# Float32 filling products, identity products tied to the dense products, and a new set of ranks in an mLSTM + two-MLP kernel

## The chip, the cores and the metric

The kernel runs on one core of a Trainium2 chip. The metric is the device time of one execution in microseconds, lower is better; the time of a kernel is the median of its runs. TensorE (PE in the profile) multiplies matrices, VectorE (DVE), ScalarE (ACT) and GpSimd (POOL) work element by element, SyncE (SP) issues the transfers. Each engine takes its own instructions strictly in their written order; between engines only semaphores order the work.

## The reference, cut to what matters

An mLSTM layer (4 batches, 8 heads, 768 steps, head size 40) is followed by two MLPs over 3072 tokens of width 320, each with 2048 hidden units:

```python
for t in range(S):
    m_new = max(f_gate + m, i_gate)
    C = exp(f_gate + m - m_new) * C + exp(i_gate - m_new) * outer(v, k)
    n = exp(f_gate + m - m_new) * n + exp(i_gate - m_new) * k
    y[t] = sigmoid(o_gate) * (C @ q) / max(abs(n @ q), 1)
x = y reshaped to (3072, 320)
h = x @ w_in;  g = where(h >= 1, h, where(h <= -1, 0, (h + 1)**2 / 4));  x = g @ w_out
h = x @ w2_in; g = maximum(h, 0)**2;                                     out = g @ w2_out
```

The MLP weights arrive as 64-bit floats and are cut into a high and a low part in the kernel.

## The kernel before

The sequence is cut into 24 chunks of 128 steps (4 batches, 6 chunks each). The attention of a chunk is: on PE the *spreads* (L507: the decay of four heads is copied to all partitions by float32 products with 36 rows), the *scores* (L540: float32, 40 rows), the *outer product* (L575) and the *reads* (L616: products of only 41 columns); on DVE the *decay* scans (L512), the *weighing* of the scores (L521), the state `C` (L585, L589), the normalised output `xn` (rc by L626 to L628, xn by L636); on ACT and POOL the gates and scalings. Then PE transposes `xn` (L655), ACT writes the high part of `xT` and DVE the low part `xTl` (L665).

Three chunks make a block, 8 blocks for each MLP. The weights are 16 tiles f. *Dense* products of a block and a tile f are `mm1` (L697, eight products of 384 columns) and, after ReLU, squaring and a split into g0 and g1 on ACT, DVE and POOL, `mm2` (L750, three products of 320 columns per chunk). The high and low parts of a weight tile are made from the raw words by ACT (L290), DVE (the shift pair L298 and L299, L303, L311) and ACT (L272). The low part of the weights is a subtraction; for the tiles in `PLO` it is done on PE as *identity products* (`plo`, twice per tile: L352 multiplies 352 float32 columns by the identity, L353 subtracts the high part), read back by ACT. All identity products write one tile in PSUM, `acc2`, which the third chunk's `mm2` needs after them.

In that same tile, *filling products* (L818, `idle`) multiply zeros. They compute nothing that is used. There are `FILL` of them, rank 1e6, so the plan puts one wherever PE would stand still.

What sets the order is a list scheduler, `Plan`. Every step has an engine (or a choice of engines), a rank and an assumed duration. The plan walks through time by its own durations, gives each free engine the ready step of lowest rank, and writes the instructions in that order. Tables of numbers set the ranks: `AT` (attention of the first nine chunks), `WAT` (weight tiles of the first MLP), `LEAD1` (later chunks), `GATE` and `GDMA` (gates of the later chunks and their transfers), `SIGL`, `WLEAD2`; `GLOV` lists the blocks whose low part of g is bound to DVE, other blocks may have it on POOL.

Of the kernel before, what the change touches and what calls it, by code (L numbers as in the profile page):

```python
# [10 lines left out]
BF16 = mybir.dt.bfloat16  # L11
# [24 lines left out]
class Plan:  # L36
# [5 lines left out]

    TABLE = {"sig": "sigmoid", "a1": "exp", "a2": "exp", "a3": "exp"}
# [14 lines left out]
    def order(self):  # L58
# [50 lines left out]
        while len(out) < n:  # L109
            t, eng = min((max(free[e], min(ready[i] for i in q)), e) for e, q in queue.items() if q)  # L110
            i = min((i for i in queue[eng] if ready[i] <= t), key=lambda i: (self.steps[i][1], i))
            queue[eng].remove(i)
            out.append((t, i))
            dur = self.steps[i][0][eng]
            want = self.TABLE.get(self.steps[i][2].__name__)
            if want and want != table:
                table, dur = want, dur + 1.3
            shared = eng == "P" or isinstance(dur, Shared)
            free[eng] = end = (max(t, port) if shared else t) + dur
            if shared:  # L120
                port = end
            for j in after[i]:
                left[j] -= 1
                lat = 0.02 if eng in self.steps[j][0] and eng != "SP" else self.LAT.get(eng, 0.1)
                ready[j] = max(ready[j], end + lat)
                if not left[j]:
                    enqueue(j)
# [34 lines left out]
AT = [-24, -19, -12, -4, 2, 2.0, 5.5, 8.5, 10.0]  # L162
WAT = [-13, -13.0, -7.5, -7.5, -3, -3.5, 1, 0.0, 6.0, 14.5, 16.0, 17.5, 16.5, 23.0, 22.5, 28.0]
LEAD1 = {3: [10.0, 11.5, 3.5], 4: [10.5, 6, 2.0], 5: [11.0, 8.0, 4.5], 6: [11.5, 7.5, 7.5], 7: [9.0, 5, 4.0]}
# [5 lines left out]
GATE = -14  # L170
FILL, FDUR = 140, 0.2
SIGL, GDMA = 3, 6
PLO = (0, 2, 3, 5, 6, 7)
WLEAD2 = (13, 0)
WDMA = 6
SGNV, LOV = (4, 4), (4, 0)
GLOV = (0, 1, 2, 3)
# [7 lines left out]
def kernel(  # L185
# [161 lines left out]
    def plo(f, rank, z):  # L347
        W, K = f"w{f}", (0, f)
        for i, (c0, c1) in enumerate(((0, WH // 2), (WH // 2, WH))):
# [10 lines left out]

            key = ("acc2", -1, f, i)
            last = plan.plo
            plan.plo = key + (1,)
            plan.add(T, rank, 0.85, sub, [("wt", K, 3), (W, 1), ("acc2", -1), ("nid", 0), last], [key])
# [446 lines left out]
    def idle_in():  # L811
        t_["idle"] = new("x2", [128, 512], BF16)
        nc.vector.memset(t_["idle"], 0.0)

    def idle(first):
        if first:
            t_["idle_ps"] = new("acc2", [128, 512])
        nc.tensor.matmul(out=t_["idle_ps"][:, WH // 2:], lhsT=t_["idle"][:, 0:128], rhs=t_["idle"][:, WH // 2:],  # L818
# [8 lines left out]
    for i in range(FILL):  # L827
        plan.add(T, -97 if i == 0 else 1e6, 0.22 if i < 30 else FDUR, lambda i=i: idle(i == 0),
# [105 lines left out]
```

## Time and profile before

| | us |
|---|---|
| median of 3 runs | 889.65 |
| lowest, highest | 886.09, 890.43 |
| the profiled execution | 887.01 |
| its span in the trace | 885.2 |
| PE busy in it | 868.0 (98%) |
| DVE, ACT, POOL busy | 468.3, 443.5, 333.1 |
| first dense product starts | 66.55 |

A busy PE is not a PE at its peak: the profile also has the clock that the chip granted to TensorE, as a share of 2.4 GHz, and only 1.00 and 0.50 (1.2 GHz) occur. In the views by stretch a mean between them is a mixture. The profile's page has the shares of the whole span; this case needs views of single stretches of its first 130 us, below.

### The profile page before, as it was taken

What the parts mean: (1) busy time and instruction counts of PE and PEld (TensorE: products, weight loads), DVE (VectorE), ACT (ScalarE), POOL (GpSimd) and SP (SyncE); (2) the same over time, 40 slices, a digit from 0 to 9 for tenths busy, and PEclk for the clock granted to TensorE, in tenths of its full rate; (3) what the DMA queues carried; (4) which work ended last, traced back from release to release, by engine and by line L of the source; (5) the groups of instructions that cost most, each with busy time, mean ns of one, the idle gap of its engine ahead of it and who ended that gap; (6) DMA issues with size and microseconds to landing.
All of it is one profiled execution on the core that took longest, in us unless ns stands there. A gap on an engine that the chain in (4) does not pass through costs nothing.

```text
span 885.2 us, 14965 instructions
## 1 busy us (share of the span) xinstructions
PE 868.0 (98%) x5782; PEld 845.9 (96%) x5782; DVE 468.3 (53%) x834; ACT 443.5 (50%) x919; POOL 333.1 (38%) x318
## 2 busy tenths in 40 slices
PE   7989999999999999999999999999999999999997
PEld 6868999999999999999999999999999999999997
DVE  4788888996765655345437788822222222222221
ACT  5255457764554554545568765533343434343433
POOL 3212431003221246446335666533333333333333
PEclk6789999999999999999999999999999999999999
DMA  6555562455441434334002333011010000000000
GB/s 202 186 180 163 172 176 88 142 171 165 124 125 47 120 106 122 108 100 124 28 10 68 131 121 126 10 34 41 26 33 26 25 26 16 8 16 9 16 9 23
DMA packets 55979, 75.72 MB, mean 86 GB/s; under 512 B 7252, under 2 KB 44792, under 8 KB 55908
## 3 DMA queue, kind: packets, MB, share of 16 engines
q1 hardware_dynamic: 55908, 74.77, 27.1%
q8 instruction: 45, 0.74, 0.3%
q14 instruction: 26, 0.21, 0.1%
HBM read 65.90 MB, written 8.85 MB: 84 GB/s over the span
## 4 chain that ended last, share of the span: by engine, by line
PE 93%; DVE 3%; DMA 2%; ACT 1%; issue 0%; SPq 0%; DVEq 0%; ACTq 0%
PE h L697 39%; PE acc L750 38%; PE v L616 4%; PE s L540 3%; PE s L655 2%; PE v L612 2%; PE v L575 1%; PE s L507 1%; PE acc L352 1%; DMA vko<-in_vko_dram 1%; DVE d L512 1%; DVE wt L303 1%; DMA qk<-in_qk_dram 0%; PE acc L818 0%; PE h L507 0%
## 5 line engine op out<-in xcount | busy, mean ns | idle before, releaser
L750 PE MATMUL acc<-w,g 128*128 128x320 f32 x2304 | 379.3, 311 | 0.0
L750 PEld LDWEIGHTS acc<-w,g 128*128 128x128 f32 x2304 | 350.6, 188 | 2.5 <-DVE o L778 0.3
L697 PE MATMUL h<-xTh,w 128*128 128x384 f32 x1280 | 351.8, 340 | 0.4 <-DVE r L715 0.3
L725 POOL TENSOR_TENSOR g<-r,g 128x384 fp32r<-128x384 f32 x192 | 204.9, 1069 | 285.0 <-ACT g L272 270.1
L697 PE MATMUL h<-xTl,w 128*128 128x384 f32 x768 | 258.8, 337 | 0.0
L697 PEld LDWEIGHTS h<-xTh,w 128*128 128x128 f32 x1280 | 233.4, 188 | 1.7 <-DVE r L715 0.9
L717 DVE TENSOR_TENSOR r<-r,h 128x384 f32<-128x384 f32 x128 | 70.8, 554 | 233.4 <-ACT r L704 233.3
L272 ACT ACTIVATE g<-r 128x384 fp32r<-128x384 f32 x256 | 133.5, 523 | 114.2 <-DVE r L717 64.3
L697 PEld LDWEIGHTS h<-xTl,w 128*128 128x128 f32 x768 | 144.8, 189 | 0.0
L704 ACT ACTIVATE r<-h 128x384 f32<-128x384 f32 x128 | 62.7, 490 | 137.3 <-PE h L697 104.6
L702 ACT ACTIVATE r<-h,half 128x384 f32<-128x384 f32 x128 | 74.1, 579 | 94.1 <-PE h L697 91.6
L715 DVE SCALAR_TENSOR_TENSOR r<-r,h 128x384 f32<-128x384 f32 x128 | 70.0, 548 | 72.6 <-ACT r L708 69.4
L708 ACT ACTIVATE r<-r 128x384 f32<-128x384 f32 x128 | 67.0, 523 | 3.0
L512 DVE TENSOR_TENSOR_SCAN d<-fb,csb 128x512 f32<-128x512 f32 x36 | 50.2, 1395 | 9.5 <-PE v L616 9.4
L547 POOL TENSOR_TENSOR vt<-vko,it 128x369 f32<-128x369 f32 x24 | 23.1, 961 | 80.0 <-PE v L616 53.6
L616 PEld LDWEIGHTS v<-vt,d 128*128 128x128 f32 x384 | 49.1, 197 | 0.5
L616 PE MATMUL v<-vt,d 128*128 128x41 f32 x384 | 49.2, 279 | 0.0
L569 POOL TENSOR_TENSOR kt<-vko,ws 128x360 f32<-128x360 f32 x19 | 16.8, 885 | 75.2 <-ACT ws L518 75.2
L725 DVE TENSOR_TENSOR g<-r,g 128x384 fp32r<-128x384 f32 x64 | 37.9, 594 | 8.7 <-ACT g L272 8.3
L521 DVE TENSOR_TENSOR d<-s,d 128x512 f32<-128x512 f32 x48 | 31.5, 680 | 17.8 <-PE s L540 17.6
L561 POOL TENSOR_TENSOR qt<-qh,ab 120x384 f32<-120x384 f32 x20 | 22.2, 1110 | 35.6 <-DMA ab<-a 28.3
L595 POOL TENSOR_TENSOR C<-cx,csb 120x369 f32<-120x369 f32 x16 | 15.4, 960 | 53.3 <-DVE cx L589 50.2
(76 smaller groups left out, 686.7 us busy)
## 6 DMA issues: line engine op xcount, KB each, us to landing
wraw<-in_wts_dram SPq DMA_DIRECT2D x32, 704.0 KB
vko<-in_vko_dram SPq DMA_DIRECT2D x24, 524.5 KB
fb<-f SPq DMA_DIRECT2D x18, 512.0 KB
qk<-in_qk_dram SPq DMA_DIRECT2D x48, 160.0 KB
x<-x SPq DMA_DIRECT2D x24, 192.0 KB
x<-o SPq DMA_DIRECT2D x24, 160.0 KB
out_dram<-o SPq DMA_DIRECT2D x24, 160.0 KB
qh<-in_qh_dram SPq DMA_DIRECT2D x20, 180.0 KB
```

The lines of the kernel that those rows point to most:

```text
L272: nc.scalar.activation(out=out, in_=in_, func=ACTF.Copy)
L512: nc.vector.tensor_tensor_scan(out=d.rearrange("p h t -> p (h t)"), data0=(z["fb"][a] if spr else z["fb"][:, 4 * a:4 * a + 4]).rearrange(" ...
L521: nc.vector.tensor_mul(out=z["d", a], in0=z["s", a], in1=z["d", a])
L616: nc.tensor.matmul(out=z["y"][:, E * h:E * (h + 1)], lhsT=z["d", a][:, h - 4 * a], rhs=z["vt"][:, h], start=(h == 0 and c == 0), stop=True ...
L697: nc.tensor.matmul(out=h, lhsT=a, rhs=b, start=(i == 0), stop=(i == 7))
L702: nc.scalar.activation(out=r, in_=z["h"], func=ACTF.Relu, scale=0.5, bias=half)
L704: nc.scalar.activation(out=r, in_=z["h"], func=ACTF.Relu)
L708: nc.scalar.activation(out=z["r"], in_=z["r"], func=ACTF.Square)
L715: nc.vector.scalar_tensor_tensor(out=r, in0=r, scalar=1.0, in1=z["h"], op0=ALU.min, op1=ALU.max)
L717: nc.vector.tensor_mul(out=r, in0=r, in1=z["h"])
L725: engine[e].tensor_sub(out=z["g1"], in0=z["r"], in1=z["g0"].bitcast(F32))
L750: nc.tensor.matmul(out=acc[k][:, 0:DM], lhsT=a, rhs=b, start=(f == f0 and i == 0), stop=(f == f1 - 1 and i == 2))
```

## The change

The filling products become float32 (100 in place of 140, still 160 columns); their duration in the plan becomes 0.17, doubled before 8 us of the plan's time (`COLD`). The identity products of a tile f of 5 or more wait, in the plan, for the dense product `mm1` of the first block with tile f - 5. `PLO` has seven tiles in place of six, `GLOV` two blocks in place of four, and the tables of ranks are set anew.

```diff
+    COLD = 8.0
...
+            if eng == "T" and t < self.COLD:
+                dur *= 2
...
-AT = [-24, -19, -12, -4, 2, 2.0, 5.5, 8.5, 10.0]
+AT = [-24, -19, -13.0, -3.5, 0.5, 2.0, 5.5, 10.5, 14.0]
...
-GATE = -14
-FILL, FDUR = 140, 0.2
-SIGL, GDMA = 3, 6
-PLO = (0, 2, 3, 5, 6, 7)
-WLEAD2 = (13, 0)
+GATE = -24
+FILL, FDUR = 100, 0.17
+SUBD = 5
+SIGL = 11
+GDMA = 59
+PLO = (0, 1, 2, 3, 4, 6, 7)
+WLEAD2 = (13, 6)
...
-GLOV = (0, 1, 2, 3)
+GLOV = (1, 3)
...
+            late = [("h", rank_of[first, f - SUBD])] if f >= SUBD else []
+            plan.add(T, rank, 0.85, sub, [("wt", K, 3), (W, 1), ("acc2", -1), ("nid", 0), last] + late, [key])
...
-        t_["idle"] = new("x2", [128, 512], BF16)
+        t_["idle"] = new("x2", [128, 288])
...
-        nc.tensor.matmul(out=t_["idle_ps"][:, WH // 2:], lhsT=t_["idle"][:, 0:128], rhs=t_["idle"][:, WH // 2:],
+        nc.tensor.matmul(out=t_["idle_ps"][:, WH // 2:], lhsT=t_["idle"][:, 0:128], rhs=t_["idle"][:, 128:288],
...
-        plan.add(T, -97 if i == 0 else 1e6, 0.22 if i < 30 else FDUR, lambda i=i: idle(i == 0),
+        plan.add(T, -97 if i == 0 else 1e6, FDUR, lambda i=i: idle(i == 0),
```

Line numbers after L270 grow by 3 to 8 (the filling products are L826, the spreads L515, the scores L548, the outer product L583, the reads L624, the transposes L663, the identity products L357 and L358). `w_403` and `w_405` are the weight tile f = 0; `acc_131` is the tile in `acc2`, `x_125` the zeros.

PE between the scores of the second chunk and the reads of that chunk. Before, where 18 filling products end (a load of the zeros and a product each):

```order
L818 MATMUL acc_131<-x_125 128x160
L655 MATMUL s<-csb,xn 128x128 x3
L575 MATMUL v<-vt,kt 120x123 x3
L507 MATMUL s<-w_119,csb 128x128 x4
L818 LDWEIGHTS x_125
L818 MATMUL acc_131<-x_125 128x160
L352 MATMUL acc_131<-wt,csb 128x352
L353 MATMUL acc_131<-w_405,nident 128x352
```

The same place in the change, from the scores on:

```order
L548 MATMUL s<-qk 128x128 x8
L826 MATMUL acc_131<-x_125 128x160 x21
L583 MATMUL v<-vt,kt 120x123 x3
L663 MATMUL s<-csb,xn 128x128 x3
L826 MATMUL acc_131<-x_125 128x160
L515 MATMUL s<-w_119,csb 128x128 x4
L826 MATMUL acc_131<-x_125 128x160 x2
L624 MATMUL v<-vt,d_276 128x41 x4
L515 MATMUL s<-w_119,csb 128x128 x4
L624 MATMUL v<-vt,d_297 128x41 x4
```

The outer product of the second chunk now stands ahead of the transposes of the first, both behind 21 filling products, and the identity products of tile 0 have moved behind the reads.

PE further on, from the identity products of tile 0 to the transposes of the second chunk, in the change:

```order
L357 MATMUL acc_131<-wt,csb 128x352
L358 MATMUL acc_131<-w_403,nident 128x352
L826 MATMUL acc_131<-x_125 128x160 x6
L357 MATMUL acc_131<-wt,csb 128x352
L358 MATMUL acc_131<-w_403,nident 128x352
L826 MATMUL acc_131<-x_125 128x160 x18
L583 MATMUL v<-vt,kt 120x123 x3
L663 MATMUL s<-csb,xn 128x128 x3
```

The outer product of the third chunk stands behind these 18 filling products; before it stood behind that chunk's scores, with no filling product directly ahead.

DVE around the second chunk's `xn`. Before:

```order
L636 TENSOR_TENSOR xn<-v,sg 128x320
L303 SCALAR_TENSOR_TENSOR wt<-wraw,wt 128x704
L298 TENSOR_SCALAR wt<-wt 128x704
L299 TENSOR_SCALAR wt<-wt 128x704
L311 SCALAR_TENSOR_TENSOR wt<-wraw,wt 128x704
L512 SCALAR_TENSOR_TENSOR d_510<-s,csb 128x512
L665 TENSOR_TENSOR xTl<-s,xTh 128x3x128
```

And in the change (L593 is the state `C` of the third chunk, which reads its outer product):

```order
L644 TENSOR_TENSOR xn<-v,sg 128x320
L316 SCALAR_TENSOR_TENSOR wt<-wraw,wt 128x704
L308 SCALAR_TENSOR_TENSOR wt<-wraw,wt 128x704
L593 TENSOR_TENSOR C<-v,csb 120x369
L316 SCALAR_TENSOR_TENSOR wt<-wraw,wt 128x704
L673 TENSOR_TENSOR xTl<-s,xTh 128x3x128
```

The state of the third chunk has moved ahead of the low part of the second chunk's `xT`, so the weight work and `xTl` behind it on DVE wait for that outer product.

## Rows read from the trace of the kernel before

**Rows 1.** The page, part 1: busy time of each engine and its share.

```profile
PE 868.0 (98%) x5782; PEld 845.9 (96%) x5782; DVE 468.3 (53%) x834; ACT 443.5 (50%) x919; POOL 333.1 (38%) x318
```

**Rows 2.** Stretches: length; PE, PEld, DVE, ACT, POOL busy; granted clock; DMA share; GB/s.

```profile
8.19:20.30 12.11, 11.85 (x65) 9.85 (x65) 4.71 (x6) 7.97 (x12) 4.70 (x5) 0.50 0.73 235
21.17:32.61 11.44, 11.44 (x59) 10.36 (x59) 6.26 (x11) 1.85 (x4) 1.94 (x3) 0.50 0.50 165
...
35.00:43.10 8.10, 7.83 (x69) 6.65 (x67) 7.91 (x15) 3.86 (x9) 1.79 (x2) 1.00 0.73 229
...
45.04:52.00 6.96, 6.96 (x35) 5.39 (x36) 4.98 (x7) 3.41 (x7) 1.51 (x1) 0.51 0.33 109
52.00:66.55 14.55, 12.21 (x87) 9.00 (x85) 13.78 (x24) 8.19 (x19) 2.13 (x2) 1.00 0.63 204
66.55:79.30 12.75, 12.75 (x97) 11.76 (x97) 11.80 (x19) 6.75 (x14) 2.92 (x3) 1.00 0.41 131
79.30:82.70 3.40, 3.40 (x12) 2.61 (x12) 2.75 (x5) 1.17 (x5) 0.79 (x1) 0.50 0.89 263
82.70:130.00 47.30, 46.45 (x361) 43.50 (x360) 40.91 (x82) 25.50 (x58) 19.39 (x18) 1.00 0.60 180
130.00:880.60 750.60, 749.06 (x4962) 741.05 (x4960) 366.07 (x649) 380.86 (x787) 293.23 (x276) 1.00 0.22 69
```

**Rows 3.** PE in order of time, filling products: start, length, what, count, idle before.

```profile
1.25 3.67 PE L818 MATMUL acc<-x 128*128 128x160 bf16 x30 [1.25 <-DVE ws L498]
...
17.98 2.32 PE L818 MATMUL acc<-x 128*128 128x160 bf16 x16
...
32.61 2.53 PE L818 MATMUL acc<-x 128*128 128x160 bf16 x18
...
41.14 1.96 PE L818 MATMUL acc<-x 128*128 128x160 bf16 x26
```

**Rows 4.** Chain that ended last: start, length, what; a float32 product is two records.

```profile
49.29 1.25 PE acc L352 x2
...
53.34 0.60 PE acc L352 x2
53.94 0.17 PE acc L353
...
55.14 0.86 PE v L616 x8
...
61.93 1.08 PE s L507 x8
...
69.60 1.09 PE s L540 x16
70.69 0.83 PE v L575 x6
```

**Rows 5.** PE in order of time: a spread, transposes of two chunks, the first dense product.

```profile
21.17 2.04 PE L507 MATMUL s<-w,csb 36*128 36x128 f32 x8 [0.88 <-DVE d L521]
...
35.41 0.53 PE L655 MATMUL s<-csb,xn 128*128 128x128 f32 x3 [0.27 <-DVE xn L636]
...
45.04 0.79 PE L655 MATMUL s<-csb,xn 128*128 128x128 f32 x3 [1.94 <-DVE xn L636]
...
66.55 0.44 PE L697 MATMUL h<-xTh,w 128*128 128x384 f32 x1
```

**Rows 6.** DVE in order of time: shift pair, rc, low part, and a weighing.

```profile
41.48 0.52 DVE L298 TENSOR_SCALAR wt<-wt 128x704 f32<-128x704 f32 x1
...
42.47 0.16 DVE L626 TENSOR_SCALAR rc<-v 128x8 f32<-128x8 f32 x1
...
43.10 0.29 DVE L320 TENSOR_TENSOR w<-wt,w 64x128 fp32r<-64x128 f32 x1
...
52.55 1.29 DVE L521 TENSOR_TENSOR d<-s,d 128x512 f32<-128x512 f32 x2 [2.07 <-PE s L540]
```

**Rows 7.** The page, part 5: the low part of g on POOL and on DVE.

```profile
L725 POOL TENSOR_TENSOR g<-r,g 128x384 fp32r<-128x384 f32 x192 | 204.9, 1069 | 285.0 <-ACT g L272 270.1
...
L725 DVE TENSOR_TENSOR g<-r,g 128x384 fp32r<-128x384 f32 x64 | 37.9, 594 | 8.7 <-ACT g L272 8.3
```

More of the change, by code (lines that the diff above doesn't have):

```diff
@@ L161 @@
 SPR = 6
-AT = [-24, -19, -12, -4, 2, 2.0, 5.5, 8.5, 10.0]
-WAT = [-13, -13.0, -7.5, -7.5, -3, -3.5, 1, 0.0, 6.0, 14.5, 16.0, 17.5, 16.5, 23.0, 22.5, 28.0]
-LEAD1 = {3: [10.0, 11.5, 3.5], 4: [10.5, 6, 2.0], 5: [11.0, 8.0, 4.5], 6: [11.5, 7.5, 7.5], 7: [9.0, 5, 4.0]}
+AT = [-24, -19, -13.0, -3.5, 0.5, 2.0, 5.5, 10.5, 14.0]
+WAT = [-15.5, -10.0, -8.0, -8.0, 0, -5.0, 1.5, 0.0, 6.5, 22.5, 30.0, 20.0, 25.5, 29.0, 27.5, 33.5]
+LEAD1 = {3: [10.5, 10.5, 2.5], 4: [14.0, 10.0, 2.0], 5: [12.0, 5.5, 2.0], 6: [14.5, 12.0, 10.5], 7: [10.5, 5.5, 4.5]}
 LEAD2 = {3: [12, 9, 3], 4: [12, 9, 6, 3]}
@@ L359, in put @@
                     copy(A, w[64:128, WL:c1], x[64:128, WL - c0:c1 - c0])
+            first = visits[0][0]
             key = ("acc2", -1, f, i)
@@ L363, in plo @@
             plan.plo = key + (1,)
-            plan.add(T, rank, 0.85, sub, [("wt", K, 3), (W, 1), ("acc2", -1), ("nid", 0), last], [key])
+            late = [("h", rank_of[first, f - SUBD])] if f >= SUBD else []
+            plan.add(T, rank, 0.85, sub, [("wt", K, 3), (W, 1), ("acc2", -1), ("nid", 0), last] + late, [key])
             plan.add(A, rank, act(352) + 0.2 * i, put, [key], [key + (1,), (W, 1, 1 + i)])
```

## The prediction

> **What bounds the kernel now.** Read first the page's busy times: PE is busy for 868.0 of 885.2 us [rows 1], so the time is PE's. Then the stretches [rows 2]: from 130.00 to 880.60 PE lacks 1.54 us of 750.60 at a clock of 1.00, and from 82.70 to 130.00 it lacks 0.85 us. There the change can gain almost nothing, since the dense products stay as they are. What can move lies ahead of the first dense product at 66.55 us [rows 5], and in one stretch behind it, 79.30 to 82.70, at a clock of 0.50 [rows 2].
>
> Ahead of 66.55 two things are lost. The filling products [rows 3] do no work. And the granted clock is 0.50 from 8.19 to 20.30, from 21.17 to 32.61 and from 45.04 to 52.00 [rows 2], which doubles a product: 352 float32 columns take 1.25 us at 0.50 and 0.60 at 1.00 [rows 4]. The reader should see that PE was not idle there: 11.44 of 11.44 us busy, at 0.50. What it did in these stretches was mostly spreads (36 rows), scores (40 rows) and reads (41 columns). The clock rose after 18 filling products in a row from 32.61 [rows 3]; it was 0.50 behind an idle time of 1.94 us at 45.04 [rows 5]; and it fell again at 79.30 with no idle time at all [rows 2], after reads and spreads.
>
> The Trainium skill, in "TensorE: Matmul & The Clock Gate", Part 1, "What's actually happening", has the clock follow how busy PE has been. The 11.44 busy microseconds at 0.50 do not agree with plain busy time as the measure. By that rule bfloat16 filling, which keeps PE just as busy, would hold the clock as well as float32 filling, and the change of type would only add the fillings' length; that is worked out as the slower rival.
>
> **The change part by part.** *The price of a filling product.* In bfloat16 it took 75 ns at full clock (26 in 1.96 us) and 145 ns at half (16 in 2.32) [rows 3]. A float32 product of 160 columns is not in the trace. From below, by columns alone: 160/352 of 0.60, so 0.27. From above: a line through the spread, 1.08 us for four products of 128 columns, so 0.27 each, and 0.60 for 352 [rows 4]; at 160 columns 0.32. I take 0.30, between them. At half clock the same line through 2.04/4 = 0.51 [rows 5] and 1.25 [rows 4] gives 0.62, the share of columns 0.57; I take 0.59. So 100 fillings cost 30 us at full clock, where 140 took 18.9 us in all at their mixed clock. The plan puts them where it expects PE to be idle, but at 0.17 us each; behind the first 20 the other 80 make PE late by up to 80 x 0.13 = 10 us against the plan. That is the cost side. The plan's own numbers are no durations and enter nothing else.
>
> *The new order carried to the first dense product*, with durations of rows 4 to 6 (spread 1.08, scores 1.09, outer product 0.83, read of four heads 0.86, identity product 0.60 + 0.17 = 0.77, three transposes 0.53), at first as if the clock stayed full.
>
> The 30 fillings before, 3.67 us, are 20 at 145 ns and 10 at 75 ns, so the clock rose at about 4.2. From 1.25 to 4.2 five float32 fillings fit, the other 15 take 4.5 us: end 8.7, against the gates' 8.19, late by 0.5. Then on PE: 9 fillings and a small transpose to 11.5, scores 12.6, 5 fillings and two spreads with one filling between to 16.6, 14 fillings to 20.8. Spread, outer product, spread, a filling and five small transposes (put at 0.5, by the three that take 0.53), read, filling, read, scores: 27.7. Before, these scores ended at 32.61, where the next filling starts [rows 3]. The full clock gains 4.9 us.
>
> Then 21 fillings, 6.3 us: 34.0; outer product 34.8; transposes 35.4. Before, the transposes started at 35.41 [rows 5]. Most of the 4.9 us is given back: `xn` would have been ready several microseconds earlier, but the transposes stand behind the fillings, and DVE's state `C`, `xTl` and weight work wait for PE too. On to the second chunk's transposes: filling, spread, two fillings, read, spread, read, identity product, 6 fillings, identity product, 18 fillings, outer product, transposes: 0.3 + 1.08 + 0.6 + 0.86 + 1.08 + 0.86 + 0.77 + 1.8 + 0.77 + 5.4 + 0.83 + 0.53 = 14.9, end 50.3; before they started at 45.04 [rows 5]. A filling, two identity products, the third chunk's scores: 53.2; before, the weighing that waited for them began at 52.55 [rows 6]. So here the change is even or slightly behind; the 5 us saved ahead of 27.7 have gone into fillings.
>
> From there it is shorter. PE has two identity products (54.8), reads (weighing 1.29 after the scores, 54.5, in time) to 56.5, two identity products to 58.0. `xn` of the third chunk: rc 0.63 and shift pair 0.99 (distances of starts [rows 6]), low part 0.3, xn 0.5, again on ACT 0.2 (these two estimated by the low part's 0.29 and its columns): 59.1. Transposes 59.6, two spreads 61.8, an identity product 62.6: first dense product. Before it was 66.55, **a lead of 4.0 us**; before, PE idled for 2.34 of 14.55 us from 52.00 on [rows 2], here for about 1.
>
> *One more tile in PLO* adds two identity products, 2 x 0.77. Nine of 14 stand ahead of the first dense product, before 8 of 12. So one more stands behind it, on PE's path: minus 0.8. Tying tiles 6 and 7 to dense products moves their products behind those of tiles 1 and 2; their rest is already counted, price nothing as long as the third chunk's `mm2` has other work ahead of it, up to 1 us if not.
>
> *GLOV*: 32 subtractions of 0.594 us leave DVE, and 1.069 each go to POOL [rows 7]. DVE is busy for 11.80 of 12.75 us behind the first dense product and POOL for 2.92 [rows 2], so there is room. PE's waits that this could remove are at most 0.85 (82.70 to 130.00); the longer subtraction could add as much. I take 0. The gates' later transfers (GDMA), SIGL, WLEAD2 and the ranks of the second MLP: 0, under 130 us of full PE [rows 2]; if that cover failed, up to 1.5.
>
> *The clock.* Two stretches in the new order hold hardly anything but reads, spreads and scores: 20.8 to 27.7 (two fillings in it) and 35.4 to 40.2 (three). In this kind of mix the clock fell at 79.30. A spell at half clock lasted 3.40 there and 6.96 at 45.04 [rows 2], which costs 1.7 or 3.5 us of PE's work. As PE is what DVE waits for up to 50 us, this counts. I take 1.7 for the first stretch and half of 1.7 for the second, 2.6; bounds 0 and 5.2. The spell of 79.30 I leave as it is, since reads and spreads stand together there again.
>
> **Sum** against the profiled 887.01: 4.0 - 0.8 - 2.6 = 0.6 less, 886.4. The median is 2.64 above this execution, the other runs lie at 886.09 to 890.43; carried over, 889.65 - 0.6 = about **889.1**.
>
> **Rivals.** A measurement of this kernel can tell about 0.5%, 4.4 us, from no change.
>
> *The clock holds.* Float32 fillings and the outer product keep it full in both stretches, a filling costs 0.27 (80 x 0.03 = 2.4 us less), and GLOV removes the 0.85: 4.0 + 2.4 + 0.85 - 0.8 = 6.4 less, 883.2. For: the stretch 35.00 to 43.10 held 1.00 with a similar mix and some identity products. Against: 79.30.
>
> *The filling takes two passes in place of four.* One pass over 352 columns takes 0.17 [rows 4], so 160 columns twice would be 0.15 (2 x 0.17 x 160/352). Then the fillings vanish from the path, and DVE bounds it: its idle time in 21.17 to 32.61, 35.00 to 43.10 and 45.04 to 66.55 is 5.18 + 0.19 + 1.98 + 0.77 = 8.1 us [rows 2], so at most 8.1 - 0.8 = 7.3 less, 882.3. Against it: 0.60 for two records of the same kind of product, about four times the 0.17. The Trainium skill, "Perfetto Trace Analysis", "Engine Utilization", gives half the output rate for its FP32_LOW_HIGH; the 0.60 does not agree.
>
> *The fillings run cold (slower).* If after 20.8 the clock falls and the float32 zeros do not raise it, the blocks of 21 and 18 fillings, which stand ahead of both outer products, cost 39 x 0.29 = 11.3 us more. Net 4.0 - 0.8 - 11.3 = 8.1 more, 897.8. It decides from about 15 us at half clock (7.5 lost) between 20 and 60 us. For it: 12 and 11 us at 0.50 with a busy PE [rows 2]; this is also the case in which the change does not do what its type is for. Against: the clock rose after bfloat16 zeros, and after identity products in float32 (before 52.00 and 82.70).
>
> **How the numbers follow.** Forecast 0.59 (its own range 885.2 to 894.1), clock holds 0.20, two passes 0.03, cold fillings 0.18. So faster 0.23, same 0.59, slower 0.18. The range reaches to 883.0 for the second case and to 896.0, into the last one.
>
> **What would show it.** Fillings: 200 records, a pair at about 0.30 us where the clock is 1.00. Clock: 1.00 from 8 to about 21, a spell of 0.50 between 21 and 32. The second chunk's scores end near 28 to 30, the transposes behind the 21 fillings start at 35 to 38, DVE waits for the outer product at both places, the first dense product comes at 62 to 66. It would be wrong if a filling were far from 0.30, if the clock held or stayed low throughout, or if PE idled by more than 2 us between the first dense product and 130 us.

## The result

The changed kernel takes 900.21 us (the median of four runs from 896.05 to 900.52) where the kernel before has 890.04: a ratio of 1.013, 95% interval 1.0097 to 1.0163. Measured again beside other runs it had 899.51 against 888.66, ratio 1.0104 (1.0062 to 1.0146). The forecast was 889.1, range 883 to 896: the kernel is slower where a small gain was forecast, and the time lies above the range. On profiled executions the forecast was 886.4 and the measurement 900.42, a miss of 14.0 us. Two single executions of the runs below had a mean granted clock of 0.65 and 0.55 (1213.48 us with bfloat16 fillings in the new order, 1442.23 us in the first run with the plan told 0.28); the ratios leave them out, and without them these two medians are 892.4 and 893.8 us.

The page of the change, part 1 (busy time and share of each engine) and the filling products' group of part 5, beside [rows 1]:

```profile
PE 885.6 (99%) x5848; PEld 865.0 (96%) x5848; DVE 463.3 (52%) x798; ACT 442.3 (49%) x922; POOL 373.2 (42%) x352
...
L826 PE MATMUL acc<-x 128*128 128x160 f32 x200 | 36.0, 339 | 2.6 <-ACT w L277 1.3
```

The span is 898.6, and PE is busy for 99% of it, so the time can be read as a ledger of PE: time in which it was not busy (span less busy time), fillings, and all other products. The other products are the same work in every kernel here (1.5 us more where seven tiles stand in PLO), so what moves in that column is half speed. All the columns come from part 1 of each page and from the fillings' group in the view of groups by line:

| us | span | not busy | fillings | other products |
|---|---|---|---|---|
| before | 885.2 | 17.2 | 18.9 | 849.1 |
| the change | 898.6 | 13.0 | 36.0 | 849.6 |

17.1 us more of fillings bought 4.2 us of idle time, and 1.0 us of half speed (849.6 less 1.5, against 849.1). That is the loss: -4.2 + 17.1 + 0.5 = 13.4. The 0.5 and the 1.0 are no larger than the difference between two traces of one kernel (849.6 and 848.7 for the change); the 17.1 is.

Where it happens is in PE's order of time (start, length, what; a float32 product is two records; in brackets the idle time before and what ended it), against [rows 3] and [rows 5]:

```profile
1.28 8.30 PE L826 MATMUL acc<-x 128*128 128x160 f32 x40 [1.28 <-DVE ws L506]
9.51 0.25 PE L451 MATMUL s<-csb,w 36*128 36x36 f32 x1
...
17.61 4.07 PE L826 MATMUL acc<-x 128*128 128x160 f32 x28
...
28.18 2.08 PE L548 MATMUL s<-qk 40*128 40x128 f32 x16
30.19 7.78 PE L826 MATMUL acc<-x 128*128 128x160 f32 x42
...
38.44 0.49 PE L663 MATMUL s<-csb,xn 128*128 128x128 f32 x3
...
47.39 1.15 PE L826 MATMUL acc<-x 128*128 128x160 f32 x6 [0.55 <-ACT w L277]
...
50.58 4.61 PE L826 MATMUL acc<-x 128*128 128x160 f32 x32 [0.74 <-ACT w L277]
...
55.67 0.49 PE L663 MATMUL s<-csb,xn 128*128 128x128 f32 x3
...
57.74 0.86 PE L357 MATMUL acc<-wt,csb 128*128 128x352 f32 x2 [0.56 <-ACT w L277]
...
61.35 0.86 PE L357 MATMUL acc<-wt,csb 128*128 128x352 f32 x2 [0.55 <-ACT w L277]
...
65.46 0.86 PE L357 MATMUL acc<-wt,csb 128*128 128x352 f32 x2 [0.55 <-ACT w L277]
...
68.02 2.07 PE L515 MATMUL s<-w,csb 36*128 36x128 f32 x8
...
73.97 0.52 PE L705 MATMUL h<-xTh,w 128*128 128x384 f32 x1
```

The fourteen fillings from 17.61 take 4.00 us from start to next start, 0.286 each: the price was right. The block of 21 takes 7.78 us, because its first part runs at half speed; the second chunk's transposes come at 55.67 (45.04 before), the first dense product at 73.97 (66.55 before). DVE shows the two waits on the outer products behind the blocks of 21 and 18, and ACT shows that the read-back of an identity product waits for the fillings put behind it into the same tile:

```profile
38.64 0.54 DVE L593 TENSOR_TENSOR C<-v,csb 120x369 f32<-120x369 f32 x1 [4.87 <-PE v L583]
...
55.87 0.54 DVE L593 TENSOR_TENSOR C<-v,csb 120x369 f32<-120x369 f32 x1 [6.25 <-PE v L583]
```

```profile
46.87 0.46 ACT L277 ACTIVATE w<-acc 128x352 fp32r<-128x352 f32 x1 [2.44 <-PE acc L826]
...
49.87 0.65 ACT L277 ACTIVATE w<-acc 128x224 fp32r<-128x224 f32 x2 [2.54 <-PE acc L826]
```

The stretches of the change, cut where the speed changes (length; PE, PEld, DVE, ACT, POOL busy; granted clock; DMA share; GB/s), beside [rows 2]:

```profile
8.00:27.50 19.50, 19.50 (x148) 17.66 (x146) 10.39 (x13) 9.43 (x17) 6.41 (x7) 0.99 0.65 214
27.50:33.90 6.40, 6.40 (x34) 6.10 (x34) 5.29 (x12) 1.80 (x4) 2.39 (x3) 0.50 0.25 71
...
44.60:47.90 3.30, 2.75 (x11) 2.21 (x10) 3.27 (x5) 0.46 (x1) 2.64 (x3) 0.55 0.21 23
47.90:68.00 20.10, 16.60 (x108) 13.14 (x106) 13.49 (x25) 10.36 (x23) 1.98 (x2) 1.00 0.55 182
68.00:78.60 10.60, 10.36 (x36) 9.30 (x35) 7.86 (x11) 5.05 (x11) 0.79 (x1) 0.52 0.40 121
...
85.50:91.90 6.40, 6.40 (x28) 5.66 (x29) 3.52 (x7) 0.97 (x4) 3.19 (x4) 0.50 0.39 131
...
95.60:98.60 3.00, 3.00 (x14) 3.00 (x13) 2.72 (x8) 1.27 (x3) 1.10 (x2) 0.50 0.74 244
...
140.00:893.00 753.00, 751.47 (x4981) 743.56 (x4980) 365.73 (x631) 380.34 (x787) 325.16 (x302) 1.00 0.22 69
```

A busy microsecond at 0.50 does half a microsecond's work, so the spells (the stretches at about 0.50) cost half their busy time: 3.2 + 1.4 + 5.2 + 3.2 + 1.5 = 14.5 us. In [rows 2] the spells of before cost 5.9 + 5.7 + 3.5 + 1.7 = 16.8. The long ones up to 32.61 are gone, and new ones stand at 27.5, 68, 85.5 and 95.6.

### The profile page after: what moved, and what is told of

Read it like the earlier page. It is cut to its first block, busy times and chain, and to the rows that moved or that the text cites. A ratio compares the mean times of both kernels' runs of the same rounds, so it can differ in the third digit from the quotient of the medians.

```text
span 898.6 us, 15135 instructions
## 1 busy us (share of the span) xinstructions
PE 885.6 (99%) x5848; PEld 865.0 (96%) x5848; DVE 463.3 (52%) x798; ACT 442.3 (49%) x922; POOL 373.2 (42%) x352
## 4 chain that ended last, share of the span: by engine, by line
PE 81%; issue 9%; POOL 6%; DVE 2%; DMA 1%; ACT 1%; POOLq 0%; SPq 0%; ACTq 0%; DVEq 0%
PE h L705 33%; PE acc L758 31%; POOL g L733 5%; PE v L624 4%; PE acc L826 4%; PE s L548 3%; PE s L663 2%; PE v L620 1%; PE v L583 1%; PE s L515 1%; PE acc L357 1%; DMA ab<-a 1%; DVE wt L308 1%; DVE wt L316 0%; POOL qt L569 0%
## 5 line engine op out<-in xcount | busy, mean ns | idle before, releaser
L733 POOL TENSOR_TENSOR g<-r,g 128x384 fp32r<-128x384 f32 x224 | 244.0, 1091 | 336.8 <-ACT g L277 305.9
L520 DVE TENSOR_TENSOR_SCAN d<-fb,csb 128x512 f32<-128x512 f32 x36 | 54.2, 1511 | 6.6 <-PE v L624 4.9
L624 PEld LDWEIGHTS v<-vt,d 128*128 128x128 f32 x384 | 48.4, 195 | 0.7
L624 PE MATMUL v<-vt,d 128*128 128x41 f32 x384 | 48.6, 277 | 0.0
L826 PE MATMUL acc<-x 128*128 128x160 f32 x200 | 36.0, 339 | 2.6 <-ACT w L277 1.3
L569 POOL TENSOR_TENSOR qt<-qh,ab 120x384 f32<-120x384 f32 x20 | 25.1, 1253 | 30.0 <-DMA ab<-a 30.0
L826 PEld LDWEIGHTS acc<-x 128*128 128x128 f32 x200 | 33.0, 219 | 4.4 <-ACT w L277 1.9
L308 DVE SCALAR_TENSOR_TENSOR wt<-wraw,wt 128x704 int32<-128x704 int32 x32 | 34.0, 1066 | 0.2
```

The source lines that it names most:

```text
L520: nc.vector.tensor_tensor_scan(out=d.rearrange("p h t -> p (h t)"), data0=(z["fb"][a] if spr else z["fb"][:, 4 * a:4 * a + 4]).rearrange(" ...
L624: nc.tensor.matmul(out=z["y"][:, E * h:E * (h + 1)], lhsT=z["d", a][:, h - 4 * a], rhs=z["vt"][:, h], start=(h == 0 and c == 0), stop=True ...
L733: engine[e].tensor_sub(out=z["g1"], in0=z["r"], in1=z["g0"].bitcast(F32))
```

## The experiments

The times are medians; each ratio is to the kernel before measured on the same chip beside it (888.6 to 889.6 us); it is not exactly the quotient of the two medians. The kernel before itself spread from 882.4 to 897.4 us in these sessions, so ratios closer than about 0.004 aren't told apart. In the ledger column stands what was not busy / fillings / other products, of the profiled execution. That is one execution, and it can lie up to about 4 us from the median (888.84 against 892.07 with two blocks out, 925.78 against 921.64 with 64 columns, 883.70 against 886.69 with 365 fine fillings); where a kernel was traced twice, a column differs by up to 1.5 us.

| run | us | ratio (95%) | ledger |
|---|---|---|---|
| before | 888.6 to 889.6 | 1 | 17.2 / 18.9 / 849.1 |
| the change (again) | 899.51 | 1.0104 (1.0062 to 1.0146) | 13.6 / 35.1 / 848.7 |
| new order, bfloat16 fillings | 893.51 | 1.0061 (1.0031 to 1.0092) | 18.1 / 14.7 / 861.2 |
| old order, float32 fillings | 895.61 | 1.0103 (1.0056 to 1.0150) | 10.7 / 44.7 / 837.5 |
| filling part alone | 894.13 | 1.0071 (1.0034 to 1.0108) | 14.2 / 32.6 / 844.5 |
| ranks alone | 891.30 | 1.0034 (1.0004 to 1.0063) | 16.0 / 19.9 / 854.0 |
| old order, four bfloat16 each | 896.25 | 1.0074 (1.0048 to 1.0100) | 10.8 / 44.6 / 840.1 |
| new order, 64 columns | 921.64 | 1.0353 (1.0302 to 1.0403) | 12.0 / 45.9 / 866.1 |
| two blocks out | 892.07 | 1.0037 (1.0011 to 1.0062) | 16.1 / 22.9 / 848.1 |
| change, plan told 0.28 | 893.04 | 1.0050 (1.0029 to 1.0070) | 13.3 / 37.6 / 840.3 |
| filling part alone, told 0.28 | 891.67 | 1.0032 (0.9987 to 1.0077) | 11.5 / 33.9 / 843.6 |
| change, 40 more fillings | 905.69 | 1.0171 (1.0135 to 1.0206) | 11.4 / 48.4 / 844.4 |
| change, old PLO | 901.41 | 1.0126 (1.0089 to 1.0164) | 12.3 / 35.9 / 852.4 |
| before, 400 fine fillings | 887.52 | 0.9985 (0.9961 to 1.0009) | 12.1 / 36.5 / 836.2 |
| before, 365 fine fillings | 886.69 | 0.9967 (0.9941 to 0.9994) | 14.6 / 32.6 / 834.7 |
| the same again | 886.65 | 0.9986 (0.9962 to 1.0009) | 14.6 / 31.9 / 836.2 |

### Taking the change apart

Type undone alone, in the new order:

```diff
-        t_["idle"] = new("x2", [128, 288])
+        t_["idle"] = new("x2", [128, 512], BF16)
```

> The changed kernel with its order of instructions kept to the letter, and only the type of the 100 filling products set back to bfloat16 (they compute nothing that is used). Lengths theory (the float32 fillings, 0.286 us each where the plan reckons 0.17, stand ahead of the outer products and hold DVE for 4.87 and 6.25 us): a filling falls to 0.075 to 0.145 us, both waits on the outer products go, the first dense product comes at 63 to 67 us instead of 73.97, and the time is 888 to 892. Clock theory (the loss is products at half clock, and float32 zeros are what holds the clock up): the clock is 0.50 in more of the stretch 8 to 52 us, which gives back most of what the short fillings save, 896 to 901. Order theory (the new ranks are worse by themselves): the two waits on DVE stay, 897 to 900.

The time is 893.51 us, between the numbers of the lengths and the clock theory; the order theory falls, since the waits on the outer products shrink to 0.74 and 1.43 us. The first dense product stands at 67.67. But the 20 fillings of the first block take 0.14 us each, the price at half clock, and the spreads and scores up to 34 us take their half-speed lengths, as do products behind 64 us:

```profile
1.25 2.85 PE L826 MATMUL acc<-x 128*128 128x160 bf16 x20 [1.25 <-DVE ws L506]
...
13.50 2.07 PE L515 MATMUL h<-w,csb 36*128 36x128 f32 x8
...
29.87 2.08 PE L548 MATMUL s<-qk 40*128 40x128 f32 x16
31.88 2.98 PE L826 MATMUL acc<-x 128*128 128x160 bf16 x21
```

The stretch from 8 to 34 us of that run (columns as above) shows a granted clock of 1.00 all the same, which is taken up below:

```profile
8.00:34.00 26.00, 25.63 (x140) 22.47 (x141) 14.04 (x22) 10.55 (x19) 8.48 (x8) 1.00 0.53 170
```

The ledger has it: fillings 21.3 us less than in the change, other products 11.6 us more. So half speed takes back more than half of what the shorter fillings save. One bfloat16 product in place of one of float32 does not hold the clock here, although PE is busy for 25.63 of those 26.00 us.

Type alone, in the old order (before, with the 140 fillings in float32):

```diff
-        t_["idle"] = new("x2", [128, 512], BF16)
+        t_["idle"] = new("x2", [128, 288])
```

> The kernel before with its order kept to the letter, and only its 140 filling products in float32 (they compute nothing that is used). Lengths theory: 140 fillings at 0.286 to 0.57 take 40 to 48 us where they took 18.9, so 21 to 29 us more of PE, less up to 10 us that a clock of 1.00 in the stretches 8 to 32 gives back; first dense product at 78 to 86 us, time 901 to 910. Clock theory: the clock stays at 1.00 from 8 us on up to the first dense product and behind it, and the saving at the scores, reads and spreads makes up for most of the longer fillings: 892 to 897. Order theory: the order is the old one, so no more than 893.

The time is 895.61 us, in the clock theory's range, above the order theory's and below the lengths theory's. PE, by start, shows full-speed lengths from the first scores to the spreads ahead of the first dense product, at 73.39:

```profile
14.54 1.16 PE L540 MATMUL s<-qk 40*128 40x128 f32 x16
...
30.16 1.16 PE L540 MATMUL s<-qk 40*128 40x128 f32 x16
31.25 5.16 PE L818 MATMUL acc<-x 128*128 128x160 f32 x36
...
72.31 1.15 PE L507 MATMUL s<-w,csb 36*128 36x128 f32 x8
73.39 0.44 PE L697 MATMUL h<-xTh,w 128*128 128x384 f32 x1
```

Full speed saves 11.6 us of other products and 6.5 of idle time, and costs 25.8 us of fillings. So enough filling does hold the clock; it costs more than it brings.

The two halves of the change: the fillings (type, number, the plan's 0.17, PE's assumed durations doubled ahead of 8 us, identity products tied to dense products) with the old tables, and the new tables with the old fillings. The tie stands in both halves, so neither run tells what it does by itself. The first differs from the change by

```diff
-AT = [-24, -19, -13.0, -3.5, 0.5, 2.0, 5.5, 10.5, 14.0]
+AT = [-24, -19, -12, -4, 2, 2.0, 5.5, 8.5, 10.0]
...
-PLO = (0, 1, 2, 3, 4, 6, 7)
+PLO = (0, 2, 3, 5, 6, 7)
```

and so on through all the tables, the second by

```diff
-    COLD = 8.0
+    COLD = 0.0
...
-FILL, FDUR = 100, 0.17
+FILL, FDUR = 140, 0.2
```

with the old fillings.

> The filling part of the change alone: 100 float32 fillings at the plan's 0.17, doubled ahead of 8 us, and the identity products tied to dense products, with all ranks, gates, PLO and GLOV of the kernel before. Lengths theory: the 80 later fillings are each 0.12 us longer than the plan thinks, 9 to 10 us late, as in the change: first dense product at 72 to 76 us, time 897 to 901. Clock theory: 22 fillings in a row late in the prologue keep the clock up to the first dense product, so it depends on the half-clock stretches, each 1.7 to 3.5 us: 891 to 897. Order theory: the old ranks, so 888 to 892.

> The other half: the new ranks, gates, PLO, GLOV and the tie to dense products, but 140 bfloat16 fillings at the plan's old figures. Lengths theory: the fillings are short again and the plan's figure for them is near the measured 0.075 to 0.145, so no outer product is held: first dense product at 64 to 68 us, time 888 to 892. Clock theory: half clock from 8 to 20 and from 21 to 32 us as in the kernel before, and one more spell behind the first dense product: 892 to 896. Order theory: the third chunk's state stands ahead of the second chunk's low part on DVE and the identity products stand back to back: 896 to 900.

The fillings alone cost 0.7%, the ranks alone 0.3%, both together 1.0 to 1.3%. The fillings alone land in the clock theory's range (894.13 in 891 to 897), and their first dense product comes at 66.39, not at 72 to 76 as the lengths theory had it: of the 13.7 us that they add, 4.6 come back in other products and 3.0 in idle time. The ranks alone land in the lengths theory's (891.30 in 888 to 892): with short fillings no outer product is held for more than 1.00 us. But their ledger shows 4.9 us more of other products, 1.5 of them the seventh tile and 3.4 half speed. That the ranks by themselves carry the loss, 896 to 900, falls.

### Type or length?

The old order with each filling replaced by four bfloat16 products in a row, so that it lasts about as long as a float32 one:

```diff
-        nc.tensor.matmul(out=t_["idle_ps"][:, WH // 2:], lhsT=t_["idle"][:, 0:128], rhs=t_["idle"][:, 128:288],
-                         start=True, stop=True)
+        for _ in range(4):
+            nc.tensor.matmul(out=t_["idle_ps"][:, WH // 2:], lhsT=t_["idle"][:, 0:128], rhs=t_["idle"][:, 352:512],
+                             start=True, stop=True)
```

> The order of the kernel before, kept to the letter as in the run with the type alone, but each of the 140 filling products is four bfloat16 products of 160 columns in a row (they compute nothing that is used), so that a filling keeps PE about as long (4 x 0.075 = 0.30 us at full clock) without being float32. Type theory (float32 zeros hold the clock and bfloat16 zeros do not): products stay at half speed in 8 to 34 us as in the kernel before, a filling takes 0.58 there, and the time is 905 to 925. Length theory (what holds the clock is how PE is filled, not the type): the same picture as with float32 fillings, full speed from 7 us on, 894 to 900.

The time is 896.25 us, in the length theory's range and far below the type theory's, and the picture is the same product for product as with float32 (first dense product at 73.65):

```profile
15.25 1.16 PE L540 MATMUL s<-qk 40*128 40x128 f32 x16
...
30.56 1.16 PE L540 MATMUL s<-qk 40*128 40x128 f32 x16
31.66 5.16 PE L819 MATMUL acc<-x 128*128 128x160 bf16 x72
...
73.65 0.44 PE L697 MATMUL h<-xTh,w 128*128 128x384 f32 x1
```

So the type does nothing for the clock that four bfloat16 products in its place do not do as well. The Trainium skill's "TensorE: Matmul & The Clock Gate", Part 1, has the clock follow how busy PE has been, and here the run agrees. The change's choice of float32 only made a filling four times as long at one go.

But PE's busy time, as the profile counts it, isn't it either. The change with fillings of 64 columns, order kept:

```diff
-        nc.tensor.matmul(out=t_["idle_ps"][:, WH // 2:], lhsT=t_["idle"][:, 0:128], rhs=t_["idle"][:, 128:288],
-                         start=True, stop=True)
+        nc.tensor.matmul(out=t_["idle_ps"][:, WH // 2:WH // 2 + 64], lhsT=t_["idle"][:, 0:128],
+                         rhs=t_["idle"][:, 128:192], start=True, stop=True)
```

> The changed kernel with its order kept to the letter, and each filling product over 64 float32 columns in place of 160 (they compute nothing that is used). A filling should take 0.12 us at full clock by its columns, so 100 take 12 us in place of 28.6. Length theory: the waits of DVE on the outer products shrink by 3.6 and 3.1 us, the first dense product comes at 64 to 67 us, and the time is 887 to 891. Clock theory (the long fillings are what keeps the clock up from 8 to 27 us): with less of them products run at half speed in more of 8 to 60 us, which takes back 5 to 8 us, 893 to 898.

The time is 921.64 us, 3.5% slower and far outside both expectations. A filling takes 0.445 us (14 in 6.23), more than the 0.286 of the long one, because products keep their half-speed lengths: spreads take 2.07 us as late as 98 us, and the lengths halve only among the dense products at about 106 us (first dense product at 103.87). From 1.28 to 65 us PE was busy without a gap:

```profile
23.24 6.23 PE L826 MATMUL acc<-x 128*128 128x64 f32 x28
...
40.21 2.08 PE L548 MATMUL s<-qk 40*128 40x128 f32 x16
42.22 9.22 PE L826 MATMUL acc<-x 128*128 128x64 f32 x42
...
98.44 3.87 PE L515 MATMUL s<-w,csb 36*128 36x128 f32 x16
```

and in the stretches of that run (columns as above):

```profile
40.00:60.00 20.00, 20.00 (x98) 19.28 (x98) 8.56 (x17) 2.00 (x5) 2.98 (x3) 1.00 0.41 125
```

Two things are to be seen there: PE is busy 20.00 of 20.00 us at half speed, as in [rows 2] at 21.17 to 32.61; and the granted clock reads 1.00 although every product in it has its half-speed length. The lengths decide here, not that column. Why fillings of 64 columns did not raise the clock, with PE as busy, no run here shows. The same edit in the old order, with 140 fillings:

> The order of the kernel before, kept to the letter, with 140 float32 fillings of 64 columns in place of 160 (they compute nothing that is used). With 160 columns the products ran at full speed from 7 us to 80 us, but the fillings took 40 us. Length theory: at 0.12 us each the fillings take 17 us, close to the 18.9 of the old bfloat16 ones; if the clock still holds, the 10 to 12 us that products at half speed cost in the kernel before are saved in part (DVE has 8 us of idle time there, which bounds it): 881 to 887. Clock theory (the short fillings do not hold it): products at half speed from 8 to 34 us as before, and nothing is saved: 888 to 893.

Its four runs lie between 913.2 and 945.3 us, so no ratio is given; all four are far outside both expectations. The trace shows the same as with the new order: fillings at 0.44 us and spreads at 2.07 up to 117 us, where the first dense products start.

### What the plan was told

The change with one number set to the measured length:

```diff
-FILL, FDUR = 100, 0.17
+FILL, FDUR = 100, 0.28
```

> The changed kernel with one number set: the plan reckons 0.28 us for a filling in place of 0.17, which is what one takes, so that it puts other work where it will really come. Plan theory (the loss is that the plan put outer products behind fillings that it thought short): blocks of 21 and 18 fillings ahead of the outer products go, DVE no longer waits 4.87 and 6.25 us there, first dense product at 64 to 67 us in place of 73.97, time 888 to 892. Ledger theory (PE is busy 98% of the time, so the time is the sum of its work, and 100 float32 fillings are still 28.6 us where the old ones were 11.2): only idle time and half-clock time that go away count, 892 to 898. Clock theory: as in the ledger, and the time is decided by how long products stay at half speed between 27 and 100 us (some 23 us in the changed kernel): each 4 us of it that go save 2.

> The same kernel as the run in which the changed kernel's plan is told 0.28 us for a filling (894.4 against 889.55 for the kernel before, and about 900 for the change), for a trace of an undisturbed execution. Ledger theory: 100 fillings are 28.6 us as in the change; the 6 us saved lie in waits of DVE on the outer products that are gone and in fewer spells at half speed ahead of the first dense product, which comes at 68 to 71 us; the spells behind it stay. Plan theory: the first dense product at 64 to 67 us, and the rest of the loss is behind it.

The time is 894.37 us the first time and 893.04 the second, whose trace is used. About 6 us of the 10 to 11 lost are back, with the same 100 fillings: 37.6 us of them, but 840.3 of other products where the change has 849.6. The time is in the ledger theory's range; the first dense product, at 66.14, is where the plan theory had it. The wait of DVE on the second chunk's outer product shrinks to 1.77 us and the other vanishes. The fillings now reach to 64 us, with six more at 83 to 87 and four at 108, instead of ending before 56, and the clock holds up to there:

```profile
62.65 1.62 PE L826 MATMUL acc<-x 128*128 128x160 f32 x10
64.20 1.15 PE L515 MATMUL s<-w,csb 36*128 36x128 f32 x8
...
66.14 0.34 PE L705 MATMUL h<-xTh,w 128*128 128x384 f32 x1
...
76.05 2.07 PE L515 MATMUL s<-w,csb 36*128 36x128 f32 x8
```

The last row is the spell behind the first dense product; the kernel before has one too, at 79.30 [rows 2]. The same edit on the filling part alone:

> The filling part alone, with the old ranks, as before (894.1, where the kernel before had 888.6), and the plan told 0.28 us for a float32 filling in place of 0.17. Its 100 fillings then stand in 19 places instead of 12, 9 to 26 of them behind 48 us, where that run had none left. Ledger theory (the time is PE's work plus its idle time plus what half speed costs; a filling is free only where PE would have idled or where it keeps the clock up): the fillings stay at 28.6 us, but the idle time ahead of the first dense product falls from 5 to 2 us, and the spells at half speed at 50 to 54 and 61 to 71 us, some 7 us of loss, go: 884 to 889. Lengths theory (float32 fillings are too long wherever they stand): no better than 892 to 895.

The time is 891.67 us, with an interval from 0.9987 to 1.0077: lower than 894.13 by the median, not lower than before. The ledger theory's 884 to 889 was too hopeful: its first dense product comes at 62.16, earlier than in any other run, yet spells from 73 to 79 and from 91 to 100 us give much of that back. So the first dense product is a poor measure of these kernels; PE's ledger is the one that adds up.

The change with the blocks of 21 and 18 fillings left out and nothing else moved:

```diff
+        t_["n_idle"] = t_.get("n_idle", -1) + 1
...
+        if 51 <= t_["n_idle"] < 72 or 81 <= t_["n_idle"] < 99:
+            return
```

> The changed kernel with its order kept, and the blocks of 21 and of 18 fillings ahead of the two outer products left out (61 of 100 fillings remain; they compute nothing that is used). Lengths theory: 39 x 0.286 = 11.2 us go from the path of DVE's two waits (4.87 and 6.25 us), first dense product at 63 to 66 us, time 889 to 892. Clock theory: the clock had fallen by 27.5 us, and it was the block of 21 that raised it at 34; without the blocks the reads, spreads and identity products up to 66 us run at half speed, some 10 to 15 us of lost work: 897 to 910.

The time is 892.07 us. The lengths theory had 889 to 892, and the first dense product at 63 to 66, where it comes at 67.59. Fillings 13.1 us less than in the change, idle time 3.1 more, other products 1.5 less: the two blocks weigh 13.1 us and bought 3.1 us of idle time. The traced execution is the fastest of ten; by the medians and ratios 6 to 8 us of the loss are back. The clock theory's 897 to 910 falls: without the block of 21, products run at half speed from 30.70 to 45 us, but there is less to run.

### The spells behind the fillings, and PLO

The change with 40 more fillings (FILL 140), which fall behind 55.67 us:

> The changed kernel with 140 float32 fillings in place of 100; the order is the same up to the transposes of the second chunk at 55.67 us, and the 40 more stand among the identity products, transposes and spreads up to the first dense product (they compute nothing that is used). Lack theory (the products from 68 to 78 us ran at half speed because no filling was left): they run at full speed, the spreads in 1.08 in place of 2.07 us, and the later spells at 85.5 and 95.6 us shrink too; 40 x 0.286 = 11.4 us more of filling against 3 to 4 us of idle time and some 6 us at half speed: 898 to 903. Order theory (reads, spreads and scores standing together let the clock fall whatever stands ahead): the spells stay, 904 to 912.

The time is 905.69 us, in the order theory's range and above the lack theory's. The spreads ahead of the first dense product (81.06) run at 1.15, so the half speed at 68 us came from fillings having run out, as the lack theory has it; but spells come back at 91 to 104, and 12.4 us more of fillings saved 5.2 of other products:

```profile
76.48 1.15 PE L515 MATMUL s<-w,csb 36*128 36x128 f32 x8
...
79.12 1.15 PE L515 MATMUL s<-w,csb 36*128 36x128 f32 x8
...
95.23 2.08 PE L548 MATMUL s<-qk 40*128 40x128 f32 x16
```

The change with the old six tiles in PLO:

```diff
-PLO = (0, 1, 2, 3, 4, 6, 7)
+PLO = (0, 2, 3, 5, 6, 7)
```

> The changed kernel with the six tiles of the old PLO in place of seven. Price by count: two identity products less, 2 x 0.77 us, so about 1.5 us less, 898 to 900, the rest as in the changed kernel. Clock theory: fewer identity products ahead of the first dense product shift what DVE and ACT wait for, and the spells at half speed at 68, 85.5 and 95.6 us move by 2 to 4 us either way: 894 to 902.

The time is 901.41 us against 899.51 for the change beside it: the intervals overlap, so the 1.5 us by count is neither shown nor ruled out. The trace shows why it can't be read: with two identity products less, third-chunk scores and reads wait for DVE at 56 and 58 us, and products run at half speed from 58.5 to 78, so the other products are 3.7 us more than in the change beside it, not 1.5 less.

> The changed kernel itself once more, beside the runs sent with it and the kernel before. Every theory expects about what the first measurement gave, a ratio of 1.010 to 1.016, some 898 to 902 where the kernel before has 889.

The time is 899.51 us and the ratio 1.0104, as every theory expected.

### Fine fillings

If the type does nothing, fillings can be short and many, and the plan can put them into gaps at their real length. The kernel before with

```diff
-FILL, FDUR = 140, 0.2
+FILL, FDUR = 400, 0.075
...
-        plan.add(T, -97 if i == 0 else 1e6, 0.22 if i < 30 else FDUR, lambda i=i: idle(i == 0),
+        plan.add(T, -97 if i == 0 else 1e6, 0.145 if i < 45 else FDUR, lambda i=i: idle(i == 0),
```

and then with 365 in place of 400, so that hardly any stands behind the first dense product:

> The kernel before with 400 bfloat16 fillings in place of 140, and the plan told what one takes, 0.145 us at first and 0.075 later (they compute nothing that is used); ranks and all else as before. Four bfloat16 fillings did for the clock what one of float32 did, so this is the same idea in finer grains. Ledger theory: 400 x 0.075 is 30 us of filling where there were 11.2, 19 more; of it 7 us stand where PE idled, and some 12 to 16 us of half-speed loss go with a clock that holds from 8 to 80 us: 885 to 891. Type theory (only float32 zeros hold the clock): products stay at half speed in 8 to 34 us, and the fillings cost more than they bring: 897 to 910.

> The kernel before with 365 fine bfloat16 fillings, the plan told their real length (0.145, then 0.075 us); with 400 it had 887.5 against 888.6, with 35 of them behind the first dense product. Ledger theory: the 35 take 2.6 us of PE where PE has other work, so without them 884 to 886.5. Clock theory: those 35 kept the clock up behind 66 us, and one more spell at half speed of 3 to 6 us, worth 1.5 to 3 us, takes the place of what they cost: 886 to 889.

> The kernel with 365 fine bfloat16 fillings once more, in more rounds. Ledger theory: its profiled execution had 14.6 us of idle PE, 32.6 of fillings and 834.7 of other products, 3.3 us less in all than the kernel before, so a ratio of 0.994 to 0.998. Chance theory (the first comparison caught good executions, and how long products stay at half speed differs from run to run by as much): 0.998 to 1.001.

The clock is up from 10 us on, by the scores and spreads of the run with 365:

```profile
8.51 2.11 PE L818 MATMUL acc<-x 128*128 128x160 bf16 x28
10.55 1.16 PE L540 MATMUL s<-qk 40*128 40x128 f32 x16
...
24.77 2.87 PE L818 MATMUL acc<-x 128*128 128x160 bf16 x39
...
62.87 0.44 PE L697 MATMUL h<-xTh,w 128*128 128x384 f32 x1
```

Other products fall by 14.4 us, fillings rise by 13.7, idle time falls by 2.6 (the 11.2 us that two expectations give for the old fillings is too low; the trace has 18.9). With 400 the time is in the ledger theory's range, and the type theory's 897 to 910 falls. With 365 the medians lie 2 us below the kernel before both times, in the ranges of the clock theory and then of the chance theory; the first interval ends at 0.9994, the second at 1.0009: 0.1 to 0.3% faster by the ratios, and that it is faster at all isn't settled. It does beat the change, by 13 us.

## Why the prediction was wrong, point by point

- **The price of a filling: right.** 0.30 forecast, 0.286 measured at full clock.
- **The order and its waits: right in place, short in size.** DVE waits for the outer products behind the blocks of 21 and 18, as carried: 4.87 and 6.25 us. The transposes were forecast at 34.8 and near 50, and came at 38.44 and 55.67, late by the points below.
- **The clock: the step that failed.** The sum let every spell ahead of 66.55 go and put 2.6 us in their place, with the spell of 79.30 (1.7) left: 4.3 us of half speed. Measured are 14.5. The two stretches that it named came to 3.2 + 1.4 = 4.6 us (from 27.5 and from 44.6), inside its upper bound of 5.2. The miss lies behind 68 us: 5.2 + 3.2 + 1.5 = 9.9 us where the sum had 1.7. It was not asked what holds the clock where no filling is left, behind 56 us. For the spell at 68 us the run with 40 more fillings shows that this was the cause; for those at 85.5 and 95.6 the cause stays open. Together that is 10.2 of the 14.0 us.
- **A term that wasn't there.** PE waits for ACT at two fillings and three identity products ahead of 66 us (0.55, 0.74, 0.56, 0.55, 0.55): 2.95 us. The carry took these products without the read-back that the next one has to wait for; the view of groups of the kernel before shows such waits too, 0.6 us at identity products and 1.6 at fillings.
- **The start.** The first 20 fillings end at 9.51, not 8.7: by the two prices of a filling (0.59 as forecast, 0.286 as measured) the clock rose near 6 us, an estimate, and not at 4.2. That is 0.8 us; in the second trace they end at 8.97. 10.2 + 2.95 + 0.8 = 13.95 of 14.0. That this comes out so closely is in part luck: the 80 later fillings alone are 80 x 0.014 = 1.1 us cheaper than forecast, which the sum leaves out.
- **The rival "fillings run cold"** came near the time (897.8) by another way: the block of 21 ran partly at half speed (7.78 us), the block of 18 did not. Only 9.7 us at half clock lie between 27.5 and 47.9, below the 15 from which it was to decide; the rest came behind 68 us.
- **"Two passes" and "the clock holds"** fall by 0.286 us a filling and by the spells.
- **The rest.** GLOV, SIGL, GDMA and WLEAD2 cost nothing that shows, as forecast: from 140.00 to 893.00 PE lacks 1.53 of 753 us. That bfloat16 would hold the clock as well and float32 only add length, which the prediction worked out by the Trainium skill's rule, is borne out in part: four bfloat16 products in place of one of float32 do hold it, one in place of one does not (the run with the type undone). Behind the failed step lies that no ledger was drawn up ahead: its own 30 us of fillings against 18.9 would have shown that the sum rests on the clock.

Shown by the runs: that four bfloat16 products do for the clock what a float32 one does; that the two blocks cost more than they bring (6 to 8 us); that telling the plan the real length brings back more than half the loss; that the half speed at 68 us came from fillings having run out. Only argued from traces: the shares of the ACT waits and the start. Open: why fillings of 64 columns did not raise the clock; what the tie does; what of the ranks' 0.3% is the seventh tile; and which order keeps the clock up behind the first dense product, where most runs have a spell between 72 and 92 us.

## What to carry to other kernels

Where an engine is busy nearly all the time, put up a ledger first: what a filling adds, what idle time it can take, and what half speed it can remove; a filling that takes more than the last two makes the kernel slower however it is placed. A planner has to be told the length that the trace shows: fillings thought 0.17 and taking 0.286 stood ahead of the work that others waited for, and were used up before 56 us, ahead of the place at 68 us where the clock fell. And fill in grains as fine as the gaps, but try each grain: four bfloat16 products of 160 columns did for the clock what a float32 one did, and 64 columns did not.

## What the runs showed of the hardware that was not expected

- Products of 64 float32 columns kept PE busy without a gap (20.00 of 20.00 us from 40 to 60) and at half speed for some 100 us, at 0.445 us a filling; with float32 products of 160 columns in the same order the lengths halved within the first block. Bfloat16 products of 160 columns, one for one, did not do that there (20 in 2.85 us); four for one, in the order of before, did.
- The granted-clock column can read 1.00 where all lengths are doubled (40 to 60 us of the 64-column run, 8 to 34 us of the run with the type undone). A spread of 2.07 or about 1.15 us tells the speed more surely.
- Filling does not secure what comes behind it: with 140 float32 fillings ahead of the first dense product at 73.39, products still took their half-speed lengths again from 86.4 to 90 us.
